# Weight conversions tied to their item and spread over the items; query and key tests loaded four steps ahead

## The chip, the cores and the metric

The kernel runs on one core of one Trainium2 chip. The metric is the device time of one launch in microseconds; before the change it is 623.04 us, the median of 3 runs (622.54 to 623.23).

## The reference

What is computed is a sparse causal attention followed by two feed-forward layers, all in float32. There are 2 batches, 8 heads, 768 positions and 64 columns a head; 1536 tokens of 512 columns enter each layer, with 2048 hidden columns.

```python
scores = q @ k.T / sqrt(D) + bias            # local window of 96 and 8 global keys
x = softmax(where(keep, scores, -1e9)) @ v   # -> 1536 x 512
h = x @ moe_w_in                             # layer 0
g = maximum(h, 0) + log1p(exp(-abs(h)))
x = g @ moe_w_out
h = x @ moe2_w_in                            # layer 1
out = (h * clip(h + 3, 0, 6) / 6) @ moe2_w_out
```

The weights arrive as 64-bit floats, which the kernel reads as pairs of 32-bit words.

## The kernel before

**Items.** Each layer's 2048 hidden columns are cut into 16 chunks of 128, and the chunks into phases of 6, 5 and 5 (PHASES). Within a phase the loop goes over three groups of 512 tokens, and within a group over the phase's chunks. One pass, a chunk times a token group, is an *item* (`item`, L362): 12 matrix products make h from x and the chunk's input weights, `split_g` (L264) applies the layer's function on ScalarE and VectorE and splits the result into a high and a low part (gh, gl), and 12 products add it into four accumulators. Each factor is a sum of two reduced-precision parts, so a product is made of three (`matmul3`, L296). An item is named by four digits: layer, phase, group, chunk within the phase. Four banks hold h, so TensorE can make the h of later items while an earlier item's g is still being formed.

**Units.** A chunk's input weights and its output weights are each one *unit*, 64 in all; wa9_1 belongs to chunk 9, half 1. `unit_load` (L186) issues the unit's 512 KB DMA into a tile raw, of which four exist. `unit_convert` (L201) turns the words into float32 and splits them: Abs on ScalarE (L219), a clamp on GpSimd (L220), three bit operations on VectorE (L221, L224, L227), a copy on ScalarE (L231, the high part), a subtraction on VectorE (L232, the low part). Twelve units are converted beside the attention in a shorter way. From unit 12 on, `run` (L457) calls `weight_step(1)` (L249) once behind each item: one more unit, if a slot for its chunk is free. Eleven slots hold weights; in a phase's last token group each item frees its chunk's slot.

**Tests.** From the second phase of layer 1 on, `run` also calls `check_step` (L730): 36 steps that test whether the inputs are in the range that this path allows. Twelve (`range_step`, L234) load a unit of weights again and reduce it on VectorE with four operations (L243 to L247); 24 load 128 rows of q or k, 256 KB, and square and sum them on ScalarE (L747). All use the tiles raw. At the end a flag is made that decides whether a general path runs again; it does not here. The last token group (`last_items`, L408) makes all its h first (hz0 to hz4), calls four test steps behind each, and only then accumulates.

**Order.** Each engine takes its instructions in program order, and that order is set when the program is built: the framework places every instruction by its own estimate of when its inputs are ready. In the attention and the products of the first layer that run beside it a table (ORDER) fixes it; behind that it is free. So a unit's work that was called behind an item may stand many items earlier in an engine's queue, as far as slots and raw tiles allow.

Of the kernel before, what the change touches and what calls it, by code (L numbers as in the profile page):

```python
# [21 lines left out]
KC = DM // P  # L22
NCH = DFF // P
PHASES = ((6, 5, 5), (6, 5, 5))
FIRST_SLOTS, MORE_SLOTS = 6, 5
CW = 512
GT, GB = 256, 512
# [23 lines left out]
def r32(ap):  # L51
    return ap.bitcast(F32)
# [81 lines left out]
class Layers:  # L134
# [6 lines left out]
    def __init__(self, ctx, tc, weights, three, xsh, xsl, out):  # L141
        self.ctx, self.tc, self.nc = ctx, tc, tc.nc
        self.weights, self.xsh, self.xsl, self.out = weights, xsh, xsl, out
        self.pool("mp", 2)
        self.pool("tp", 5)
        self.pool("pp", 1)
        self.part = [self.pp.tile([P, 4, GB], F32, name=f"part{g}") for g in range(T // GB)]
        self.three = three
        self.W, self.raws, self.slot = {}, {}, {}
        self.done, self.loaded = 0, 0  # L150
        first = range(PHASES[0][0])
        early = range(2 * EARLY_PAIRS)
        self.order = [(j, u) for js in (early, first[len(early):]) for u in range(2) for j in js]
        self.order += [(j, u) for j in range(len(first), 2 * NCH) for u in range(2)]
        self.free, self.h_tags, self.acc_tags, self.wr = [], [], [], []
        self.room, self.hint, self.bare = None, False, 0
        self.plan, self.mark = None, lambda label, made: made
        self.n_h, self.halves, self.in_first, self.beside = 0, 0, True, False
        self.grow(0, FIRST_SLOTS, 2, 2)
# [41 lines left out]
    def unit_convert(self, x):  # L201

        nc = self.nc
        j, u = self.order[x]
        if u == 0:
            self.slot[j] = self.free.pop(0)
            wp, t = self.slot[j]
            self.W[j] = [wp.tile([P, CW], F32R, tag=f"w{i}_{t}", name=f"w{i}_{j}") for i in range(4)]
        raw = self.raws.pop(x)
        hi, lo = raw[:, :, 1], raw[:, :, 0]  # L210
        z = self.home(x, 6)
        if z < 4:
            a = self.part[2][:, z, :]
        else:
            a = self.wr[x % len(self.wr)].tile([P, CW], F32, tag="wa", name=f"wa{j}_{u}")
        ai = a.bitcast(I32)
        bare = x < self.bare
        if not bare:
            nc.scalar.activation(a, raw.bitcast(F32)[:, :, 1], AF.Abs)  # L219
            nc.gpsimd.tensor_scalar(out=a, in0=a, scalar1=W_HI, scalar2=W_LO, op0=ALU.min, op1=ALU.max)  # L220
        self.mark(f"u{x}.0", nc.vector.tensor_scalar(  # L221
            out=ai, in0=hi if bare else ai, scalar1=3, scalar2=0x3FFFFFF8, op0=ALU.logical_shift_left, op1=ALU.bitwise_and
        ))
        self.mark(f"u{x}.1", nc.vector.scalar_tensor_tensor(  # L224
            out=ai, in0=hi, scalar=-2 ** 30, in1=ai, op0=ALU.bitwise_and, op1=ALU.bitwise_or
        ))
        self.mark(f"u{x}.2", nc.vector.scalar_tensor_tensor(  # L227
            out=ai, in0=lo, scalar=29, in1=ai, op0=ALU.logical_shift_right, op1=ALU.bitwise_or
        ))
        wh, wl = self.W[j][2 * u:2 * u + 2]  # L230
        self.mark(f"w{x}", nc.scalar.copy(wh, a))  # L231
        self.mark(f"u{x}.3", nc.vector.tensor_tensor(out=wl, in0=a, in1=r32(wh), op=ALU.subtract))  # L232

    def range_step(self, x, m):  # L234

# [126 lines left out]
    def item(self, layer, ph, G, s):  # L362

        nc = self.nc
        xsh, xsl, part = self.xsh[G], self.xsl[G], self.part[G]
        W = self.W[layer * NCH + sum(PHASES[layer][:ph]) + s]
        wih, wil = (t.rearrange("p (k c) -> p k c", k=KC) for t in W[0:2])
        woh, wol = W[2:4]
        n = f"{layer}{ph}{G}{s}"
        h = self.h_bank(f"h{n}")  # L370
        for call in self.matmul3(
            h, [((wih[:, c], wil[:, c]), (xsh[:, c, :], xsl[:, c, :])) for c in range(KC)], True, True
        ):
            call()
        gh, gl = self.split_g(layer, h, n)
        first_s, last_s = s == 0, s == PHASES[layer][ph] - 1
        first_ph, last_ph = ph == 0, ph == len(PHASES[layer]) - 1
        if first_s:
            self.acc = [self.bank(t, f"acc{n}{i}") for i, t in enumerate(self.acc_tags)]
        for m in range(4):  # L380
            ms = slice(m * P, (m + 1) * P)
            acc, pm = self.acc[m], part[:, m, :]
            if layer == 0:
                pair = ((woh[:, ms], wol[:, ms]), (gh, gl))
            else:
                pair = ((gh[:, ms], gl[:, ms]), (woh, wol))
            for call in self.matmul3(acc, [pair], first_s, last_s):
                call()
            if not last_s:
                continue  # L390
            if layer == 0:
                if first_ph:
                    nc.scalar.copy(pm, acc)
                    continue
                nc.vector.tensor_tensor(out=pm, in0=acc, in1=pm, op=ALU.add)
                if last_ph:
                    nc.scalar.copy(xsh[:, m, :], pm)
                    nc.vector.tensor_tensor(out=xsl[:, m, :], in0=pm, in1=r32(xsh[:, m, :]), op=ALU.subtract)
                continue
            if first_ph:  # L400
                nc.scalar.mul(pm, acc, 1.0 / 6.0)
                continue
            nc.vector.scalar_tensor_tensor(out=pm, in0=acc, scalar=1.0 / 6.0, in1=pm, op0=ALU.mult, op1=ALU.add)
            if last_ph:
                t0 = G * GB + m * P
                nc.sync.dma_start(out=self.out[t0:t0 + P, :], in_=pm)

    def last_items(self, ph, G, spare_step):  # L408
# [3 lines left out]
        if self.hint:  # L412
            self.tc.mark_branch_hint_location("redo", engines=list(mybir.ALL_ENGINES))
        g, W = [], []
        for s in range(PHASES[1][ph]):
            W.append(self.W[NCH + sum(PHASES[1][:ph]) + s])
            wih, wil = (t.rearrange("p (k c) -> p k c", k=KC) for t in W[s][0:2])
            h = self.h_bank(f"hz{s}")
            for call in self.matmul3(
                h, [((wih[:, c], wil[:, c]), (self.xsh[G][:, c, :], self.xsl[G][:, c, :])) for c in range(KC)], True, True  # L420
            ):
                call()
            wp, t = self.free.pop(0)
            where = [wp.tile([P, CW], F32R, tag=f"w{i}_{t}", name=f"g{i}_{s}") for i in range(2)]
            g.append(self.split_g(1, h, f"z{s}", where))
            for _ in range(4):
                spare_step()
        for m in range(4):
            acc = self.bank(self.acc_tags[m], f"accz{m}")
            t0 = G * GB + m * P  # L430
# [26 lines left out]
    def run(self, att=None, spare_step=lambda: None):  # L457
# [32 lines left out]
        self.plan, self.mark = None, lambda label, made: made  # L490
        self.grow(1, MORE_SLOTS, 2, 2)
        self.in_first = False
        for layer in range(2):
            for ph, chunks in enumerate(PHASES[layer]):
                for G in range(T // GB - 1 if layer == 0 and ph == 0 else 0, T // GB):
                    if layer == 1 and ph == len(PHASES[1]) - 1 and G == T // GB - 1:
                        self.last_items(ph, G, spare_step)
                        continue
                    for s in range(chunks):
                        self.item(layer, ph, G, s)  # L500
                        if G == T // GB - 1:
                            self.release(layer, ph, (s,))
                        self.weight_step(1)
                        if layer == 1 and ph:
                            spare_step()


# [17 lines left out]
def fast_path(tc, ident, three, nf, counts, q, k, qt, kt, v, weights, out, flag):  # L525


    with ExitStack() as ctx, ExitStack() as actx:
# [196 lines left out]
                return step["v"] == quads  # L725

        chk = {}
        todo = list(range(-layers.bare, 2 * B * NB))

        def check_step():  # L730

            if not todo:
                return
            fp = layers.wr[1]
            if not chk:
                chk["sq"] = fp.tile([P, 2 * B * NB], F32, name="sq")
                chk["wm"] = fp.tile([P, layers.bare, 2], F32, name="wm")
            sq, wm = chk["sq"], chk["wm"]
            t = todo.pop(0)
            if t < 0:  # L740
                layers.range_step(t + layers.bare, wm)
                return
            z, n = divmod(t, B * NB)
            x = layers.wr[t % 2].tile([P, CW, 2], I32, tag="raw", name=f"chk{t}").bitcast(F32)
            x = x.rearrange("p c t -> p (c t)")[:, 0:DM]
            nc.sync.dma_start(out=x, in_=(q, k)[z][n * P:(n + 1) * P, :])
            nc.scalar.activation(x, x, AF.Square, accum_out=sq[:, t:t + 1])  # L747
            if todo:
                return
            m1 = fp.tile([P, 1], F32, name="m1")  # L750
            nc.vector.tensor_reduce(out=m1, in_=sq, axis=AX.X, op=ALU.max)
# [217 lines left out]
```

## Time and profile before

| what | value |
|---|---|
| median of 3 runs | 623.04 us |
| profiled execution, its own time | 622.77 us |
| its span (first to last instruction) | 621.0 us |
| TensorE busy | 611.2 us, 98% of the span |
| VectorE, ScalarE, GpSimd busy | 447.7, 375.0, 136.2 us |
| granted TensorE clock, mean | 0.999 |

The profiled execution lies 0.27 us under the median; 1.77 us of its time lie around the span. Busy time of TensorE is modelled: products are pipelined, and one of 512 columns is shown as 0.39 us long, while the next may start much sooner. Whether TensorE loses time is therefore read from the starts of its products, or from how many of them start in a window. On the other engines too the next instruction may start a little before the one shown ends.

### The profile page before, as it was taken

Reading aid. Unit: us, or ns where it says so; the run is one execution under the profiler, and the core shown is the slowest. Engines: PE = TensorE matmul, PEld = TensorE weight load, DVE = VectorE, ACT = ScalarE, POOL = GpSimd, SP = SyncE. Lnnn points to the kernel's source line nnn. Section 1 sums busy time; section 2 is a strip of 40 time slices with the busy share of each in tenths; the row PEclk is TensorE's granted clock in tenths of the full one; section 3 lists DMA queues with packets and bytes.
Section 4 is the critical chain, followed back from the end, with each engine's and each line's share of the span. In section 5 each row is a group of like instructions: output and inputs, shape, how many; then the busy total and the mean of one; then the engine's idle time right before and its main releaser. Section 6 shows DMA issues by size and latency. Waiting matters only on the chain.

```text
span 621.0 us, 9444 instructions
## 1 busy us (share of the span) xinstructions
PE 611.2 (98%) x3350; PEld 507.4 (82%) x3352; DVE 447.7 (72%) x945; ACT 375.0 (60%) x795; POOL 136.2 (22%) x169
## 2 busy tenths in 40 slices
PE   8999999999999999999999999999999999999997
PEld 4789888999778887888888888888888878888886
DVE  8989676649999999999878995226999442424162
ACT  6998689676887977786767752326545642222230
POOL 3855344434233333332001410001100000000000
PEclk9999999999999999999999999999999999999999
DMA  8583203014533433323101341001656610001011
GB/s 267 184 284 112 73 1 112 6 57 170 169 117 121 136 136 102 103 102 109 61 0 35 101 137 69 0 1 40 200 196 207 188 52 0 1 0 69 0 69 70
DMA packets 26803, 59.90 MB, mean 96 GB/s; under 512 B 2688, under 2 KB 9344, under 8 KB 26752
## 3 DMA queue, kind: packets, MB, share of 16 engines
q1 hardware_dynamic: 26752, 59.26, 28.6%
q8 instruction: 27, 0.44, 0.3%
q14 instruction: 24, 0.20, 0.1%
HBM read 56.10 MB, written 3.15 MB: 95 GB/s over the span
## 4 chain that ended last, share of the span: by engine, by line
PE 66%; DVE 18%; DMA 8%; ACT 4%; issue 3%; POOL 0%; SPq 0%; ACTq 0%; POOLq 0%
PE acc L301 23%; PE h L301 21%; PE hf L301 5%; PE accf L301 3%; PE s L629 3%; PE px L683 3%; PE ptp L665 3%; DVE wa L227 3%; DVE wa L224 3%; PE accz L301 2%; DMA chk<-in_q 2%; DMA chk<-in_k 2%; PE hz L301 2%; DVE w L232 2%; DVE gl L293 2%
## 5 line engine op out<-in xcount | busy, mean ns | idle before, releaser
L301 PE MATMUL h<-xsh,w 128*128 128x512 f32 x632 | 167.3, 390 | 0.9 <-DVE t L285 0.8
L301 PEld LDWEIGHTS h<-xsh,w 128*128 128x128 f32 x632 | 118.0, 188 | 27.3 <-DVE t L285 3.1
L220 POOL TENSOR_SCALAR wa<-wa 128x512 f32<-128x512 f32 x52 | 70.2, 1354 | 240.7 <-ACT wa L219 240.6
L301 PE MATMUL acc<-w,gh 128*128 128x512 f32 x344 | 106.0, 389 | 0.0
L301 PE MATMUL acc<-gh,w 128*128 128x512 f32 x288 | 92.0, 390 | 0.2 <-ACT gh L292 0.2
L293 DVE TENSOR_TENSOR gl<-t,gh 128x512 fp32r<-128x512 f32 x79 | 55.0, 696 | 48.4 <-ACT gh L292 48.3
L301 PE MATMUL h<-xsl,w 128*128 128x512 f32 x316 | 86.7, 389 | 0.0
L292 ACT CAST gh<-t 128x512 fp32r<-128x512 f32 x79 | 49.0, 620 | 56.2 <-PE acc L301 38.0
L301 PEld LDWEIGHTS acc<-w,gh 128*128 128x128 f32 x344 | 64.6, 188 | 13.4
L290 ACT ACTIVATE t<-h,three 128x512 f32<-128x512 f32 x43 | 29.5, 687 | 72.3 <-PE h L301 70.5
L291 DVE SCALAR_TENSOR_TENSOR t<-t,h 128x512 f32<-128x512 f32 x43 | 29.4, 684 | 55.9 <-ACT t L290 55.8
L301 PEld LDWEIGHTS h<-xsl,w 128*128 128x128 f32 x316 | 59.2, 188 | 12.4
L301 PE MATMUL acc<-w,gl 128*128 128x512 f32 x172 | 67.2, 391 | 1.3 <-DVE gl L293 1.3
L520 POOL TENSOR_SCALAR pm<-pm,rs 128x256 f32<-128x256 f32 (+1 forms) x96 | 57.0, 609 | 43.6 <-DVE rs L518 25.4
L301 PEld LDWEIGHTS acc<-gh,w 128*128 128x128 f32 x288 | 53.9, 188 | 12.4 <-ACT gh L292 1.0
L301 PE MATMUL acc<-gl,w 128*128 128x512 f32 x144 | 56.0, 389 | 0.0
L640 ACT ACTIVATE pm<-pm,nm 128x256 f32<-128x256 f32 (+1 forms) x96 | 46.6, 488 | 3.5 <-DVE nm L635 3.5
L219 ACT ACTIVATE wa<-raw 128x512 f32<-128x512 f32 x52 | 35.0, 673 | 14.6 <-DVE w L232 6.0
L635 DVE CUSTOM_DVE_ANT_0 pm<-s,bias 128x256 f32<-128x256 f32 (+1 forms) x96 | 35.1, 394 | 10.2 <-PE s L629 9.9
L231 ACT CAST w<-wa 128x512 fp32r<-128x512 f32 x56 | 34.5, 617 | 12.4 <-PE acc L301 8.7
L301 PE MATMUL accf<-ghf,w 128*128 128x256 f32 x192 | 41.8, 299 | 0.0
L232 DVE TENSOR_TENSOR w<-wa,w 128x512 fp32r<-128x512 f32 x56 | 38.8, 695 | 3.3 <-ACT w L231 3.3
(122 smaller groups left out, 1032.5 us busy)
## 6 DMA issues: line engine op xcount, KB each, us to landing
raw<-in_w2i SPq DMA_DIRECT2D x16, 512.0 KB, 3.2
raw<-in_w2o SPq DMA_DIRECT2D x16, 512.0 KB, 3.2
raw<-in_w1i SPq DMA_DIRECT2D x14, 512.0 KB, 4.0
raw<-in_w1o SPq DMA_DIRECT2D x12, 512.0 KB, 3.2
V<-in_v SPq DMA_DIRECT2D x12, 256.0 KB, 3.4
range<-in_w1i SPq DMA_DIRECT2D x6, 512.0 KB, 4.0
range<-in_w1o SPq DMA_DIRECT2D x6, 512.0 KB, 3.9
chk<-in_q SPq DMA_DIRECT2D x12, 256.0 KB, 3.1
```

The costliest lines, as they stand in the source:

```text
L219: nc.scalar.activation(a, raw.bitcast(F32)[:, :, 1], AF.Abs)
L220: nc.gpsimd.tensor_scalar(out=a, in0=a, scalar1=W_HI, scalar2=W_LO, op0=ALU.min, op1=ALU.max)
L231: self.mark(f"w{x}", nc.scalar.copy(wh, a))
L232: self.mark(f"u{x}.3", nc.vector.tensor_tensor(out=wl, in0=a, in1=r32(wh), op=ALU.subtract))
L290: nc.scalar.activation(t1, hf, AF.Relu, bias=self.three[:, 0:1])
L291: nc.vector.scalar_tensor_tensor(out=t3, in0=t1, scalar=6.0, in1=hf, op0=ALU.min, op1=ALU.mult)
L292: mark(f"h{n}", nc.scalar.copy(gh, t3))
L293: mark(f"L{n}", nc.vector.tensor_tensor(out=gl, in0=t3, in1=r32(gh), op=ALU.subtract))
L301: return self.nc.tensor.matmul(out, lhsT=a, rhs=b, start=start and z == 0, stop=stop and z == len(seq) - 1, **kw)
L520: mark("N", nc.gpsimd.tensor_scalar(out=t, in0=t, scalar1=rs[:, j:j + 1], scalar2=0.0, op0=ALU.mult, op1=ALU.add))
L635: mark(f"T{k}.{z}", nc.vector.tensor_tensor_reduce(out=pmz, in0=ps[z % 2][:, z // 2, 0:nsl, :].rearrange("p s t -> p (s t)"), in1=bias[:, ...
L640: mark(f"e{k}.{z}", nc.scalar.activation(pmz, pmz, AF.Exp, bias=nm[:, z:z + 1], scale=-1.0, accum_out=sm[:, z:z + 1]))
```

## The change

A unit's Abs (L219 of the kernel before) and the square of a q or k test are given an order behind the first of the 12 products of the item that they were called behind. This is no wait on the chip: no semaphore is added, it only keeps the build from placing them further ahead. A rule (`wanted`) lets a unit be called only when its share of the items up to the phase that needs it has passed: one per item in the first 15 items, then about two in three, with layer 1's last ones one per item again. Test steps begin when all units are done. Range tests and q/k tests alternate, and a q or k load is asked for four q/k steps before its square.

```diff
@@ unit_convert
-            nc.scalar.activation(a, raw.bitcast(F32)[:, :, 1], AF.Abs)
+            made = nc.scalar.activation(a, raw.bitcast(F32)[:, :, 1], AF.Abs)
+            if self.anchor:
+                self.behind(made, self.anchor)
...
+    def behind(self, made, one):
+        info = mybir.DependencyInfo(mybir.DependencyClass.NoSync, mybir.DependencyReason.DATA)
+        self.tc.add_manual_dep(made.ins, one.name, info, reason="order")
@@ item, and last_items for each hz
-            call()
+            made = call()
+            self.anchor = self.anchor or made.ins
@@ run
+        items = [(layer, ph, G, s) for layer in range(2) for ph, c in enumerate(PHASES[layer])
+                 for G in range(T // GB) for s in range(c)]
+        dues = [(k, 2 * (layer * NCH + sum(PHASES[layer][:ph]) + s + 1) + 1)
+                for k, (layer, ph, G, s) in enumerate(items) if G == 0 and s == PHASES[layer][ph] - 1]
+        def wanted(*item):
+            k = items.index(item) + 1
+            for (a, m), (b, n) in zip(dues, dues[1:]):
+                if a <= k < b and items[b][:2] <= (1, 0):
+                    return m + (n - m) * (k - a) / (b - a)
+            return 4 * NCH
...
+                        self.anchor = None
                         self.item(layer, ph, G, s)
...
-                        self.weight_step(1)
-                        if layer == 1 and ph:
+                        self.weight_step(1 if self.done < wanted(layer, ph, G, s) else 0)
+                        if layer == 1 and ph and self.done == 4 * NCH:
                             spare_step()
@@ check_step
-        todo = list(range(-layers.bare, 2 * B * NB))
+        ranges, todo, asked = list(range(layers.bare)), list(range(2 * B * NB)), []
...
-            t = todo.pop(0)
-            if t < 0:
-                layers.range_step(t + layers.bare, wm)
+            if ranges and 2 * B * NB - len(todo) >= layers.bare - len(ranges):
+                layers.range_step(ranges.pop(0), wm)
                 return
...
+            while todo and len(asked) < CHECK_AHEAD:
+                t = todo.pop(0)
...
+                nc.sync.dma_start(out=x, in_=(q, k)[z][n * P:(n + 1) * P, :])
+                asked.append((t, x))
+            t, x = asked.pop(0)
+            made = nc.scalar.activation(x, x, AF.Square, accum_out=sq[:, t:t + 1])
+            if layers.anchor:
+                layers.behind(made, layers.anchor)
```

How queues change is shown at three places; line numbers of the new program are 3 to 29 higher.

VectorE between the low parts of items 0021 and 0022, before (t1 to t3 are `split_g`'s tiles; w1 and w3 are the low parts of a chunk's input and output weights):

```order
L293 TENSOR_TENSOR gl0021_2365<-t30021_2367,gh0021_2364 128x512
L224 SCALAR_TENSOR_TENSOR wa11_0_2865<-raw11_0_2704,wa11_0_2865 128x512
L221 TENSOR_SCALAR wa10_1_2808<-wa10_1_2808 128x512
L227 SCALAR_TENSOR_TENSOR wa10_0_2759<-raw10_0_2598,wa10_0_2759 128x512
L232 TENSOR_TENSOR w3_9_2656<-wa9_1_2706,w2_9_2655 128x512
L288 TENSOR_TENSOR t30022_2416<-t30022_2416,t20022_2417 128x512
L227 SCALAR_TENSOR_TENSOR wa11_0_2865<-raw11_0_2704,wa11_0_2865 128x512
L282 SCALAR_TENSOR_TENSOR t20023_2470<-t20023_2470,t10023_2468 128x512
L285 SCALAR_TENSOR_TENSOR t30023_2469<-h0023_16_2453,t30023_2469 128x512
L224 SCALAR_TENSOR_TENSOR wa10_1_2808<-raw10_1_2651,wa10_1_2808 128x512
L232 TENSOR_TENSOR w1_10_2756<-wa10_0_2759,w0_10_2755 128x512
L293 TENSOR_TENSOR gl0022_2414<-t30022_2416,gh0022_2413 128x512
```

and now:

```order
L301 TENSOR_TENSOR gl0021_2365<-t30021_2367,gh0021_2364 128x512
L230 SCALAR_TENSOR_TENSOR wa8_0_2547<-raw8_0_2390,wa8_0_2547 128x512
L296 TENSOR_TENSOR t30022_2416<-t30022_2416,t20022_2417 128x512
L227 SCALAR_TENSOR_TENSOR wa8_1_2600<-raw8_1_2439,wa8_1_2600 128x512
L290 SCALAR_TENSOR_TENSOR t20023_2470<-t20023_2470,t10023_2468 128x512
L293 SCALAR_TENSOR_TENSOR t30023_2469<-h0023_16_2453,t30023_2469 128x512
L235 TENSOR_TENSOR w1_8_2544<-wa8_0_2547,w0_8_2543 128x512
L224 TENSOR_SCALAR wa9_0_2657<-wa9_0_2657 128x512
L230 SCALAR_TENSOR_TENSOR wa8_1_2600<-raw8_1_2439,wa8_1_2600 128x512
L301 TENSOR_TENSOR gl0022_2414<-t30022_2416,gh0022_2413 128x512
```

Before, VectorE worked here at units of chunks 9, 10 and 11; now at those of chunks 8 and 9, and two rows fewer stand between the two low parts.

ScalarE in the tests, before, items 1111 to 1113 (sq takes a square's sum):

```order
L292 CAST gh1111_5281<-t31111_5284 128x512
L290 ACTIVATE t11112_5323<-h1112_74_5308,three_70 128x512
L747 ACTIVATE chk11_5965,sq_5023<-chk11_5965 128x512
L747 ACTIVATE chk13_6038,sq_5023<-chk13_6038 128x512
L290 ACTIVATE t11113_5363<-h1113_75_5348,three_70 128x512
L747 ACTIVATE chk15_6044,sq_5023<-chk15_6044 128x512
L747 ACTIVATE chk17_6071,sq_5023<-chk17_6071 128x512
L292 CAST gh1112_5321<-t31112_5324 128x512
L747 ACTIVATE chk19_6077,sq_5023<-chk19_6077 128x512
L747 ACTIVATE chk21_6104,sq_5023<-chk21_6104 128x512
L292 CAST gh1113_5361<-t31113_5364 128x512
```

and now, items 1114 to 1123:

```order
L300 CAST gh1114_5375<-t31114_5378 128x512
L298 ACTIVATE t11120_5421<-h1120_77_5406,three_70 128x512
L776 ACTIVATE chk2_5237,sq_5187<-chk2_5237 128x512
L300 CAST gh1120_5419<-t31120_5422 128x512
L298 ACTIVATE t11121_5461<-h1121_78_5446,three_70 128x512
L300 CAST gh1121_5459<-t31121_5462 128x512
L298 ACTIVATE t11122_5501<-h1122_79_5486,three_70 128x512
L776 ACTIVATE chk3_5239,sq_5187<-chk3_5239 128x512
L300 CAST gh1122_5499<-t31122_5502 128x512
L298 ACTIVATE t11123_5537<-h1123_80_5522,three_70 128x512
L300 CAST gh1123_5535<-t31123_5538 128x512
```

Between two casts (gh) stood two to four squares; now it is one or none, and a square's load is asked for four squares earlier.

VectorE in the range tests, before, items 1102 and 1103 (wm takes the maxima):

```order
L293 TENSOR_TENSOR gl1102_5094<-t31102_5096,gh1102_5093 128x512
L246 SCALAR_TENSOR_TENSOR rangea10_5471<-rangea10_5471 128x512
L243 TENSOR_SCALAR rangea7_5343<-range7_5341 128x512
L247 TENSOR_REDUCE wm_5024<-rangea8_5383 128x1
L246 SCALAR_TENSOR_TENSOR rangea5_5263<-rangea5_5263 128x512
L293 TENSOR_TENSOR gl1103_5146<-t31103_5148,gh1103_5145 128x512
L247 TENSOR_REDUCE wm_5024<-rangea10_5471 128x1
L244 TENSOR_REDUCE wm_5024<-rangea7_5343 128x1
L291 SCALAR_TENSOR_TENSOR t31104_5196<-t11104_5195,h1104_71_5180 128x512
L247 TENSOR_REDUCE wm_5024<-rangea5_5263 128x1
```

and now, items 1114 and 1120:

```order
L255 TENSOR_REDUCE wm_5188<-rangea1_5277 128x1
L251 TENSOR_SCALAR rangea3_5357<-range3_5355 128x512
L301 TENSOR_TENSOR gl1114_5376<-t31114_5378,gh1114_5375 128x512
L252 TENSOR_REDUCE wm_5188<-rangea3_5357 128x1
L254 SCALAR_TENSOR_TENSOR rangea3_5357<-rangea3_5357 128x512
L255 TENSOR_REDUCE wm_5188<-rangea3_5357 128x1
L251 TENSOR_SCALAR rangea5_5481<-range5_5479 128x512
L252 TENSOR_REDUCE wm_5188<-rangea5_5481 128x1
L299 SCALAR_TENSOR_TENSOR t31120_5422<-t11120_5421,h1120_77_5406 128x512
L254 SCALAR_TENSOR_TENSOR rangea5_5481<-rangea5_5481 128x512
L255 TENSOR_REDUCE wm_5188<-rangea5_5481 128x1
L301 TENSOR_TENSOR gl1120_5420<-t31120_5422,gh1120_5419 128x512
```

Before, the operations of four range tests were mixed with those of the items; now a test's first operation stands right behind the last of the test before it, and the items' operations behind that.

## Rows read from the trace of the kernel before

**Rows 1.** The page, span and busy time by engine.

```profile
span 621.0 us, 9444 instructions
PE 611.2 (98%) x3350; PEld 507.4 (82%) x3352; DVE 447.7 (72%) x945; ACT 375.0 (60%) x795; POOL 136.2 (22%) x169
```

**Rows 2.** Windows of 20 us; columns: stretch, length, busy (instructions) per engine, clock, DMA.

```profile
156.00:176.00 20.00, 19.55 (x83) 15.06 (x83) 19.07 (x33) 16.30 (x30) 4.11 (x5) 1.00 0.49 158
176.00:196.00 20.00, 20.00 (x89) 16.24 (x88) 20.00 (x35) 16.03 (x28) 6.73 (x5) 1.00 0.37 127
...
216.00:236.00 20.00, 19.98 (x88) 16.06 (x86) 19.62 (x34) 15.16 (x27) 7.12 (x5) 1.00 0.31 105
236.00:256.00 20.00, 19.41 (x84) 15.56 (x84) 20.00 (x36) 15.83 (x28) 9.08 (x4) 1.00 0.40 132
...
416.00:436.00 20.00, 20.00 (x89) 16.54 (x89) 12.22 (x21) 11.44 (x20) 1.85 (x3) 1.00 0.16 53
...
476.00:496.00 20.00, 20.00 (x90) 16.57 (x89) 10.54 (x19) 13.65 (x36) 0.00 (x0) 1.00 0.60 184
496.00:516.00 20.00, 18.74 (x82) 14.81 (x81) 8.56 (x16) 7.87 (x17) 0.00 (x0) 1.00 0.14 41
```

**Rows 3.** Who waited for whom, TensorE: total us, times, longest.

```profile
PE acc L301 <- DVE gl L293: 1.3, 2, 0.7
PE h L301 <- DVE t L285: 0.8, 2, 0.6
...
PE accf L301 <- DVE glf L293: 0.4, 1, 0.4
```

**Rows 4.** The chain that ended last, in order of time: start, us, what.

```profile
245.54 2.72 PE acc L301 x12
```

**Rows 5.** VectorE, groups by shape, 160 to 300 us.

```profile
L224 DVE SCALAR_TENSOR_TENSOR wa<-raw,wa 128x512 int32<-128x512 int32 x31 | 21.8, 704 | 0.0
...
L282 DVE SCALAR_TENSOR_TENSOR t<-t,t 128x512 f32<-128x512 f32 x27 | 18.8, 697 | 0.8 <-ACT t L281 0.8
```

**Rows 6.** VectorE in order of time; columns: start, duration, instruction, [idle before].

```profile
152.25 0.68 DVE L293 TENSOR_TENSOR glf<-t3f,ghf 128x512 fp32r<-128x512 f32 x1
...
164.43 0.68 DVE L285 SCALAR_TENSOR_TENSOR t<-h,t 128x512 f32<-128x512 f32 x1
165.03 0.68 DVE L227 SCALAR_TENSOR_TENSOR wa<-raw,wa 128x512 int32<-128x512 int32 x1
...
170.43 0.41 DVE L221 TENSOR_SCALAR wa<-wa 128x512 int32<-128x512 int32 x1
170.77 0.68 DVE L293 TENSOR_TENSOR gl<-t,gh 128x512 fp32r<-128x512 f32 x1
```

**Rows 7.** ScalarE in order of time, same columns.

```profile
493.75 0.67 ACT L290 ACTIVATE t<-h,three 128x512 f32<-128x512 f32 x1
495.25 0.63 ACT L747 ACTIVATE chk<-chk 128x512 f32<-128x512 f32 x1 [0.83 <-DMA chk<-in_k]
...
496.64 0.63 ACT L747 ACTIVATE chk<-chk 128x512 f32<-128x512 f32 x1 [0.67 <-DMA chk<-in_k]
...
497.27 0.60 ACT L292 CAST gh<-t 128x512 fp32r<-128x512 f32 x1
```

**Rows 8.** TensorE in order of time, around the same stall.

```profile
498.65 0.50 PE L301 MATMUL acc<-w,gl 128*128 128x512 f32 x1 [0.60 <-DVE gl L293]
```

**Rows 9.** TensorE in order of time, first full item.

```profile
155.82 1.09 PE L301 MATMUL h<-xsl,w 128*128 128x512 f32 x4
```

**Rows 10.** The tile chk: waits for it, and issue to landing.

```profile
  ACT chk L747: 13.1, 14
...
DMA to landing us min/median/max: 2.5/2.8/4.0
```

**Rows 11.** The tile range: issue to landing.

```profile
DMA to landing us min/median/max: 3.1/4.0/5.1
```

**Rows 12.** The tile raw: issue to landing.

```profile
DMA to landing us min/median/max: 3.1/3.2/7.7
```

More of the change, by code (lines that the diff above doesn't have):

```diff
@@ L24 @@
 PHASES = ((6, 5, 5), (6, 5, 5))
+CHECK_AHEAD = 4
 FIRST_SLOTS, MORE_SLOTS = 6, 5
@@ L155, in __init__ @@
         self.free, self.h_tags, self.acc_tags, self.wr = [], [], [], []
-        self.room, self.hint, self.bare = None, False, 0
+        self.room, self.hint, self.bare, self.anchor = None, False, 0, None
         self.plan, self.mark = None, lambda label, made: made
@@ L421, in last_items @@
             ):
-                call()
+                made = call()
+                self.anchor = self.anchor or made.ins
             wp, t = self.free.pop(0)
@@ L427, in last_items @@
                 spare_step()
+            self.anchor = None
         for m in range(4):
@@ L499, in run @@
                     for s in range(chunks):
+                        self.anchor = None
                         self.item(layer, ph, G, s)
@@ L727, in fast_path @@
         chk = {}
-        todo = list(range(-layers.bare, 2 * B * NB))
+        ranges, todo, asked = list(range(layers.bare)), list(range(2 * B * NB)), []
         def check_step():
-            if not todo:
+            if not todo and not asked:
                 return
@@ L738, in check_step @@
             sq, wm = chk["sq"], chk["wm"]
-            t = todo.pop(0)
-            if t < 0:
-                layers.range_step(t + layers.bare, wm)
+            if ranges and 2 * B * NB - len(todo) >= layers.bare - len(ranges):
+                layers.range_step(ranges.pop(0), wm)
                 return
[L743 to L748, printed above, removed]
+            while todo and len(asked) < CHECK_AHEAD:
+                t = todo.pop(0)
+                z, n = divmod(t, B * NB)
+                x = layers.wr[t % 2].tile([P, CW, 2], I32, tag="raw", name=f"chk{t}").bitcast(F32)
+                x = x.rearrange("p c t -> p (c t)")[:, 0:DM]
+                nc.sync.dma_start(out=x, in_=(q, k)[z][n * P:(n + 1) * P, :])
[4 more added lines that the diff above has]
+                layers.behind(made, layers.anchor)
+            if todo or asked:
                 return
```

## The prediction

> **What bounds the kernel now.** I began with the page: TensorE is busy in 611.2 of 621.0 us [rows 1], so there seems to be nothing to gain but 10 us. Behind the attention every product of 512 columns has the same rhythm: 12 in 2.72 us [rows 4], 0.2267 us each, so that an item of 24 takes 5.44 us. At this rhythm a window of 20 us shows 89 or 90 products (the one cut at its edge included), as in 476 to 496 [rows 2]; of the 22 windows from 156 to 596 us 15 show 90 and seven fewer. The clock is at its upper level, 2.4 GHz, throughout (1.00 in each of these rows). So only missing starts can be won back, and they lie in two places [rows 2]:
>
> - 156 to 256 us: 83, 89, 89, 88 and 84 products; against 90 that is 7 + 1 + 1 + 2 + 6 = 17, or 17 x 0.2267 = 3.85 us (196 to 216 reads as 176 to 196). A wait of 0.4 us just before (accf for glf, [rows 3]) belongs to it: 4.2 us.
> - 496 to 516 us: 82, so 8 x 0.2267 = 1.8 us.
>
> Together 6.0 us. A window can read one off by where it is cut (416 to 436 shows 89 and has no wait), so I give that sum 0.5 us either way.
>
> The list of waits names what ends them [rows 3]: VectorE's gl, its t (the read that frees a bank of h), and glf. In the first place VectorE is busy 19 to 20 of 20 us [rows 2], an operation of 512 elements every 0.60 us and the integer shift every 0.34 [rows 6]. A unit costs it 0.34 + 3 x 0.60 = 2.14 us, an item of layer 0 4 x 0.60 = 2.4: together 4.54 of the 5.44 that TensorE needs, so one unit an item would fit. But between 160 and 300 us it begins 31 units for 27 items [rows 5], and they do not wait their turn: the queue was filled with units of chunks that are far from needed, and the item's own four operations stand behind them. In the second place VectorE is not busy (8.56 of 20). ScalarE is held up there: the square at 496.64 waited 0.67 us for its DMA, the one before 0.83, and the cast of gh behind them ran only at 497.27 [rows 7], so that TensorE waited 0.60 for gl [rows 8]. Squares waited 13.1 us for DMA in all [rows 10].
>
> **Part 1: units behind their item's first product, and spread.** No instruction is added or dropped; 52 units and their 52 DMAs stay. What moves: in VectorE's queue, from the last operation of the first products (glf at 152.25 [rows 6]) to the low part of item 0112, stood 152 operations, 89 of them units'; now 127, 63 of them units'. Those 25 fewer are at 0.57 us ((0.34 + 3 x 0.60) / 4 is 0.54, an item's 0.60) some 14 us taken out of the 89 us that end with the wait near 241, where TensorE lost most at once. They come back between 256 and 420 us, where VectorE had idle time in the old run (12.22 of 20 in 416 to 436 [rows 2]) and TensorE loses nothing. Of the waits in this place I therefore expect all to go: **-4.2 us**. The bounds: nothing, if the queue is late for another reason; 4.2 is all that there is.
>
> What is late next? Weights. The nearest case is chunk 10, whose input half is needed by item 0104. In TensorE's new queue 176 products lie between the first of item 0021 (155.82 + 8 x 0.2267 = 157.6 [rows 9]) and the first of 0104: 39.9 us, 197.5. In VectorE's new queue 66 operations lie between glf and that chunk's low part, 10 at 0.34 and 56 at 0.60: 37.0 us behind 152.85, 189.9. That leaves 7.6 us for its waits on ScalarE, GpSimd and DMA. Chunks 11 and later have over 20 us. A raw tile is asked for three units, some 16 us, ahead and lands in 3.2 (median) to 7.7 us [rows 12], so SP's queue, in which loads now stand in order of units, is no limit. On GpSimd only the 52 clamps move.
>
> The Trainium skill, Perfetto Trace Analysis, "Optimization Strategy", speaks against this part: where an engine has gaps one should "determine how to make those dependencies start sooner, or complete faster", and the tie makes a unit's start later. The trace does not agree with that section of the Trainium skill here: where units start soonest, TensorE waits [rows 2, 3]. By the rule the time would be that of the fourth rival below.
>
> **Part 2: squares with loads asked for early.** A load of q or k lands in 2.8 us (2.5 to 4.0 [rows 10]); four steps are about four items, 21.8 us. In the new queue of ScalarE a square stands between a cast and the next, each 0.63 us (496.64 to 497.27 [rows 7]), and no longer waits: **-1.8 us**. Bounds: 0 and 1.8. Squares come bunched only at the end: the last 15, called four behind each hz. Eight of them stand ahead of the cast for item 1214. The first four have their data; the second four are asked for as the first are done, at least 5 us before ScalarE reads h of 1214. From the end of that h TensorE has 43 products, 9.7 us, before it needs gl; Relu, four squares, cast and subtraction take 0.67 + 4 x 0.63 + 0.60 + 0.68 = 4.5. Cover: 5 us. The last squares stand ahead of the cast for hz1, whose h ends 46 products (10.4 us) before the flag's transpose in TensorE's new queue, and item outputs that stand behind q/k loads in SP's queue end nothing.
>
> **Part 3: range tests, now in a row.** Each next load waits until VectorE has read the last one. At items 1113 to 1121 four run in series: Relu and square (0.67 + 0.63), four times landing L and a first operation of 0.34, then five of 0.60 up to gl of 1121: 5.7 + 4 L. TensorE needs that gl 110 products, 24.9 us, behind the end of h of 1113. So up to L = 4.8 us nothing waits; it was 4.0 (3.1 to 5.1 [rows 11]). I take 0; with 5.1 each time it costs 1.2 us.
>
> **Sum.** 622.77 - 4.2 - 1.8 = 616.8 us for the profiled execution; the median stood 0.27 us above it, so **617.0 us**.
>
> **Rivals.**
> 1. *The ramp keeps its waits.* From 152 to 176 us four raw tiles, GpSimd and the first units are chained whatever their order; then the 7 products (1.59 us) and 0.4 us stay, 2.0 us: 619.0. For it: this is the window that loses most [rows 2], and it stands at the start of the units. Against: the new queue has glf ahead of all full units.
> 2. *VectorE stays late* in the whole first stage, as unit and item still fill 4.54 of 5.44 us; only the squares gain: 623.04 - 1.8 = 621.2. Against: the 25 operations that went.
> 3. *Order is all that changes, and the waits come back elsewhere*: no gain, 623.0. The queue rows speak against it.
> 4. *Weights come late.* Were VectorE's queue 10 us late by its waits instead of under 7.6, item 0104 waits 2.4 us: 619.4. Against: this is the one chunk with so little lead. The rule of the Trainium skill named above points to this case.
> 5. *Slower: range loads in series.* VectorE stands still behind each, with gl and t of items in its queue. Beyond L = 4.8 us each load costs four times the excess; at 7.7 us (the longest raw load [rows 12]) 5.7 + 30.8 - 24.9 = 11.6 us: 628.6. It decides from 5.7 + 4 L = 24.9 + 7.3, L = 6.6 us. Against: 5.1 was the longest of twelve, at a DMA share of 0.60 [rows 2].
>
> **How the numbers follow.** Forecast 0.60, ramp 0.18, VectorE late 0.08, no gain 0.05, weights 0.05, slower 0.04. The forecast's own bounds are 616.5 to 617.5; the range takes in the ramp and the weights, to 619.4, and 0.1 below: 616.4 to 619.4. A measurement tells 0.2%, 1.25 us, from no change; under 621.8 is faster. That is the first three cases and the weights, 0.91; I say 0.90, with 0.06 for within 0.2% and 0.04 for slower.
>
> **What would show it.** Right: windows of 20 us with 89 or 90 products from 160 to 590 us; VectorE with idle time before 256 us; squares with no DMA wait ahead of a cast that TensorE waits for; about 615 us of span. Wrong: products missing in 156 to 176 (rival 1), waits of h on L235's low part w (rival 4), idle VectorE ended by a DMA of range with TensorE waiting for gl (rival 5).

## The result and the profile after

| | before | with the change |
|---|---|---|
| median | 623.13 us (6 runs, 622.54 to 624.51) | 616.85 us (6 runs, 616.23 to 618.25) |
| ratio | | 0.9899, 95% interval 0.9883 to 0.9915 |
| profiled execution, its own time | 622.77 us | 617.12 us |
| its span | 621.0 us | 615.3 us |
| first product into a full-size h, start | 147.73 us | 147.91 us |
| last product, start | 616.51 us | 610.76 us |
| between the two | 468.77 us | 462.85 us |

The forecast was 617.0 us. The last row of the table is the yardstick of what follows: it leaves out the attention, where the change moves nothing but a few operations of units at its end, and which alone varies by 2 us from one execution to another (below). It shrank by 5.92 us; the prediction counted 6.0 us of missing starts.

The page after, span and busy time, beside [rows 1]:

```profile
span 615.3 us, 9412 instructions
PE 607.8 (99%) x3352; PEld 507.9 (83%) x3352; DVE 454.9 (74%) x945; ACT 371.2 (60%) x795; POOL 117.1 (19%) x169
```

VectorE's busy time did not fall, it rose by 7 us. The work is the same; where it stands in the queue is not.

Windows of 20 us after, in the columns of [rows 2]:

```profile
156.00:176.00 20.00, 20.00 (x90) 16.56 (x89) 19.47 (x32) 17.87 (x32) 6.79 (x6) 1.00 0.31 105
176.00:196.00 20.00, 20.00 (x90) 16.53 (x90) 19.49 (x34) 16.47 (x29) 8.05 (x4) 1.00 0.30 106
...
216.00:236.00 20.00, 20.00 (x90) 16.57 (x89) 18.56 (x31) 13.04 (x22) 2.84 (x3) 1.00 0.24 79
236.00:256.00 20.00, 20.00 (x90) 16.57 (x89) 15.37 (x26) 12.62 (x23) 1.28 (x2) 1.00 0.15 54
...
416.00:436.00 20.00, 20.00 (x90) 16.56 (x89) 14.76 (x24) 10.33 (x19) 2.90 (x4) 1.00 0.27 99
...
476.00:496.00 20.00, 20.00 (x90) 16.57 (x89) 8.90 (x16) 5.17 (x9) 0.00 (x0) 1.00 0.09 30
496.00:516.00 20.00, 20.00 (x90) 16.57 (x89) 16.88 (x29) 6.80 (x13) 0.00 (x0) 1.00 0.39 133
```

Every window has its 89 or 90 products, where [rows 2] had 83, 84 and 82 in the three worst. VectorE is still busy 19.5 of 20 us from 156 to 216, so a nearly full VectorE alone was not what cost the time. What moved is the place of the items' operations in its queue. The gl of item 0025 and the first product that reads it, before:

```profile
198.08 0.68 DVE L293 TENSOR_TENSOR gl<-t,gh 128x512 fp32r<-128x512 f32 x1
```

```profile
200.16 0.39 PE L301 MATMUL acc<-gl,w 128*128 128x512 f32 x1
```

and now:

```profile
191.33 0.68 DVE L301 TENSOR_TENSOR gl<-t,gh 128x512 fp32r<-128x512 f32 x1
```

```profile
195.31 0.39 PE L309 MATMUL acc<-gl,w 128*128 128x512 f32 x1
```

It was the 75th VectorE operation behind glf and is the 63rd. Its lead, from its end to that product, grew from 1.4 to 3.3 us.

Who waited for whom, TensorE, after, beside [rows 3]:

```profile
PE s L655 <- DMA qT<-in_qt: 1.3, 1, 1.3
PE warm L808 <- DVE zeros L576: 1.3, 1, 1.3
PE ptp L691 <- ACT pm L666: 0.3, 1, 0.3
PE ptp L691 <- ACT pT L693: 0.2, 1, 0.2
```

gl, t and glf are gone from the list; what is left belongs to the start and the attention.

### The profile page after: what moved, and what is told of

The parts are those of the page before. It is cut to its first block, busy times and chain, and to the rows that moved or that the text cites. A ratio compares the mean times of both kernels' runs of the same rounds, so it can differ in the third digit from the quotient of the medians.

```text
span 615.3 us, 9412 instructions
## 1 busy us (share of the span) xinstructions
PE 607.8 (99%) x3352; PEld 507.9 (83%) x3352; DVE 454.9 (74%) x945; ACT 371.2 (60%) x795; POOL 117.1 (19%) x169
## 4 chain that ended last, share of the span: by engine, by line
PE 96%; ACT 2%; DMA 1%; issue 0%; SPq 0%; DVE 0%
PE h L309 35%; PE acc L309 35%; PE hf L309 6%; PE accf L309 6%; PE px L709 4%; PE s L655 3%; PE ptp L691 3%; PE accz L309 2%; PE hz L309 2%; ACT pm L666 1%; DMA qT<-in_qt 1%; ACT pT L693 0%; PE warm L808 0%; SPq L582 0%; SPq L581 0%
## 5 line engine op out<-in xcount | busy, mean ns | idle before, releaser
L223 POOL TENSOR_SCALAR wa<-wa 128x512 f32<-128x512 f32 x52 | 50.0, 963 | 263.3 <-ACT wa L220 259.8
L309 PE MATMUL acc<-gh,w 128*128 128x512 f32 x288 | 93.5, 389 | 0.0
L546 POOL TENSOR_SCALAR pm<-pm,rs 128x256 f32<-128x256 f32 (+1 forms) x96 | 58.3, 623 | 42.5 <-DVE rs L544 24.0
L227 DVE SCALAR_TENSOR_TENSOR wa<-raw,wa 128x512 int32<-128x512 int32 x53 | 38.4, 725 | 0.7
```

The lines of the kernel that those rows point to most:

```text
L227: self.mark(f"u{x}.1", nc.vector.scalar_tensor_tensor(out=ai, in0=hi, scalar=-2 ** 30, in1=ai, op0=ALU.bitwise_and, op1=ALU.bitwise_or))
L309: return self.nc.tensor.matmul(out, lhsT=a, rhs=b, start=start and z == 0, stop=stop and z == len(seq) - 1, **kw)
L546: mark("N", nc.gpsimd.tensor_scalar(out=t, in0=t, scalar1=rs[:, j:j + 1], scalar2=0.0, op0=ALU.mult, op1=ALU.add))
```

## The experiments

All ratios are to the kernel before, run on the same chip beside the kernel. "Length" is the last row of the table above, taken from the one profiled execution of each. By the starts of its products the kernel before lost 4.0 us in the first place (up to 256 us) and 1.9 us in the second (near 500).

| kernel | ratio (95% interval) | length, us |
|---|---|---|
| before | 1 | 468.77 |
| the change | 0.9899 (0.9883 to 0.9915) | 462.85 |
| the change again | 0.9925 (0.9901 to 0.9950) | 462.85 |
| a_tie: units' tie alone | 0.9934 (0.9916 to 0.9953) | 463.47 |
| b_spread: spreading alone | 1.0017 (1.0002 to 1.0033) | 471.23 |
| c_tests: tests' part alone | 0.9972 (0.9959 to 0.9986) | 466.21 |
| f_sqfree: without the squares' tie | 0.9975 (0.9954 to 0.9996) | 465.09 |
| d_ask1: loads not asked early | 0.9916 (0.9894 to 0.9937) | 462.85 |
| j_ties: the two ties alone | 0.9916 (0.9895 to 0.9936) | 462.85 |
| dose1: +1 VectorE operation a unit | 0.9929 (0.9910 to 0.9948) | 464.33 |
| dose3: +3 VectorE operations a unit | 1.0346 (1.0324 to 1.0369) | 489.79 |
| range2: range loads twice as long | 0.9945 (0.9925 to 0.9964) | 463.35 |
| k_late: tie 2.5 us later | 0.9923 (0.9897 to 0.9948) | 462.96 |
| lat3: units slower on GpSimd | 1.0418 (1.0385 to 1.0451) | 494.07 |

### Which part wins the first place

**a_tie**, the kernel before with the edit below (`behind`, and the lines that set the anchor, are as in the change and left out here):

```diff
-            nc.scalar.activation(a, raw.bitcast(F32)[:, :, 1], AF.Abs)
+            made = nc.scalar.activation(a, raw.bitcast(F32)[:, :, 1], AF.Abs)
+            if self.anchor:
+                self.behind(made, self.anchor)
```

> Only the tie of the units; no spreading, tests as before. Theory A (the tie alone wins the first place, since it takes 23 of the units' operations out of VectorE's queue between glf and the low part of item 0112, 66 instead of 89, where the full change has 63): TensorE's products of 156 to 256 us come back, 4.2 us; the squares still stand two to eight between casts, so the 1.8 us near 500 stay: 618.9 us, ratio 0.993. Rival B (the spreading wins it): 623.1, ratio 1.000.

**b_spread**, the kernel before with the edit below (`wanted` is as in the change and left out here):

```diff
-                        self.weight_step(1)
-                        if layer == 1 and ph:
+                        self.weight_step(1 if self.done < wanted(layer, ph, G, s) else 0)
+                        if layer == 1 and ph and self.done == 4 * NCH:
```

> Only the spreading of the units over the items (tests in their old order, begun when the units are done); no tie. VectorE's queue has 153 operations, 89 of them units', between glf and the low part of item 0112, as before. Theory A: no gain, 623.1 us, ratio 1.000, products missing in 156 to 256 us as before. Rival B: 618.9, ratio 0.993.

Windows of a_tie:

```profile
156.00:176.00 20.00, 20.00 (x90) 16.57 (x89) 19.50 (x33) 17.85 (x31) 6.80 (x6) 1.00 0.29 105
...
236.00:256.00 20.00, 20.00 (x90) 16.57 (x89) 18.43 (x31) 13.87 (x25) 2.40 (x4) 1.00 0.23 80
...
496.00:516.00 20.00, 19.71 (x87) 15.98 (x86) 8.06 (x17) 10.00 (x24) 0.00 (x0) 1.00 0.32 97
```

and of b_spread:

```profile
156.00:176.00 20.00, 19.65 (x84) 15.27 (x83) 19.28 (x33) 16.51 (x29) 3.92 (x5) 1.00 0.48 158
...
236.00:256.00 20.00, 19.43 (x83) 15.37 (x84) 20.00 (x35) 15.91 (x28) 9.17 (x4) 1.00 0.37 132
...
496.00:516.00 20.00, 17.37 (x75) 13.74 (x75) 7.96 (x15) 8.52 (x18) 0.00 (x0) 1.00 0.18 54
```

The tie alone brings back every product of the first place. Near 500 us it keeps a loss of 0.6 us, where 1.8 were expected to stay: the kernel is 5.3 us shorter and not 4.2, and the ratio, which came out at the expected 0.993, does not show that difference. The spreading alone brings back none in the first place and loses more near 500 (two waits for gl, 2.6 us; squares wait 17.2 us for their loads instead of 13.1); why it loses more there was not followed up. A rule on when a unit is *called* won nothing here while the build could still place the called unit further ahead.

### Which part wins the second place

**c_tests**, the change without the units' tie and with one unit an item, as before; tests begin in the second phase (`@@ run` marks a cut):

```diff
-            made = nc.scalar.activation(a, raw.bitcast(F32)[:, :, 1], AF.Abs)
-            if self.anchor:
-                self.behind(made, self.anchor)
+            nc.scalar.activation(a, raw.bitcast(F32)[:, :, 1], AF.Abs)
@@ run
-                        self.weight_step(1 if self.done < wanted(layer, ph, G, s) else 0)
-                        if layer == 1 and ph and self.done == 4 * NCH:
+                        self.weight_step(1)
+                        if layer == 1 and ph:
```

> Only the tests: alternating, loads asked for four steps ahead, squares tied; units as before. Theory A: the 1.8 us near 500 go and the 4.2 us of 156 to 256 stay: 621.3 us, ratio 0.997; no cast of gh behind a square that waited for its DMA. Rival (the range tests in series take the gain back): 623.1 or above, with TensorE waiting for gl while VectorE waits for range. Tests begin five items earlier here than in the full change, while units still run.

It went as the theory has it near 500 us: ratio 0.9972, and no missing product after 242 us. The first place keeps most of its loss, 3.4 us instead of 4.0:

```profile
156.00:176.00 20.00, 19.82 (x87) 15.62 (x86) 19.93 (x34) 16.73 (x29) 4.47 (x5) 1.00 0.45 156
```

By the tiles' names, the first 169 operations behind glf on VectorE and behind ghf on ScalarE stand in the order of the kernel before. In the trace of the kernel before VectorE waits there once for ScalarE, in that of c_tests it does not:

```profile
162.61 0.69 DVE L232 TENSOR_TENSOR w<-wa,w 128x512 fp32r<-128x512 f32 x1 [0.90 <-ACT w L231]
```

So a kernel's waits can differ by some 0.6 us from one execution to another, and a difference of that size between two lengths is not by itself the effect of an edit.

**f_sqfree**, the change with

```diff
-            if layers.anchor:
-                layers.behind(made, layers.anchor)
```

in the test step, 

> The whole change without the tie of the squares; loads are still asked for four steps ahead. ScalarE's queue has one to five squares between casts again, four and five of them at items 1110 and 1111. Theory C (what won the second place is that squares no longer bunch, and the tie does that): squares wait for DMA ahead of casts again, up to 1.8 us lost, 617.5 to 618.7 us. Rival D (the early asking does it): 616.9 us, no wait of TensorE after 440 us.

**d_ask1**, the change with

```diff
-CHECK_AHEAD = 4
+CHECK_AHEAD = 1
```

> The whole change with each q or k load asked for right ahead of its square (one step instead of four); the squares keep their tie, one between two casts up to item 1212. Theory C (the tie spreads the squares, and SP issues each load as soon as a tile is free, so it lands in 2.8 us long before the square's turn): as the changed kernel, ratio 0.990, no wait of TensorE after 440 us. Rival D (the early asking is needed): squares wait for DMA at most steps, and up to 1.8 us come back, ratio 0.993.

f_sqfree asks for its loads four steps early and waits for them more than the kernel before did. The tile chk in f_sqfree, who waited for it (us, times):

```profile
  ACT chk L776: 22.6, 15
```

ScalarE in f_sqfree, in order of time, as [rows 7]:

```profile
509.31 0.63 ACT L776 ACTIVATE chk<-chk 128x512 f32<-128x512 f32 x1 [1.21 <-DMA chk<-in_k]
...
510.81 0.63 ACT L776 ACTIVATE chk<-chk 128x512 f32<-128x512 f32 x1 [0.78 <-DMA chk<-in_k]
...
511.44 1.12 ACT L300 CAST gh<-t 128x512 fp32r<-128x512 f32 x2
```

and TensorE there, as [rows 8]:

```profile
512.82 0.50 PE L309 MATMUL acc<-w,gl 128*128 128x512 f32 x1 [1.75 <-DVE gl L301]
```

Five squares stand between the cast before, at 503.18, and this one. There are four tiles raw: once four loads are under way, the next one has to wait for a square (this is read from the code and not measured). With the tie and without early asking (d_ask1) squares wait 1.7 us in all, in three places, and TensorE never. So the tie of the squares won the second place, and asking early won nothing measurable. With that tie the change, c_tests, d_ask1 and j_ties lose nothing there. Without it the loss is 0.6 us (a_tie), 1.9 (before), 2.2 (f_sqfree) or 3.2 (b_spread): what it is worth depends on where the rest stands.

**j_ties**, the kernel before with the units' tie of a_tie and, in the test step (what sets the anchor is again left out),

```diff
-            nc.scalar.activation(x, x, AF.Square, accum_out=sq[:, t:t + 1])
+            made = nc.scalar.activation(x, x, AF.Square, accum_out=sq[:, t:t + 1])
+            if layers.anchor:
+                layers.behind(made, layers.anchor)
```

> The kernel before with the two ties alone: no spreading, range tests first and in a row of twelve, loads not asked for early. Theory: VectorE's queue has 66 units' operations up to the low part of 0112 and one or two squares stand between two casts, so both places are won: ratio 0.990, some 617 us. Rival (the other parts are needed to keep the tests from bunching): the range tests now stand twelve in a row among items 1100 to 1113, and TensorE waits there for gl, 1 to 3 us: ratio 0.992 to 0.995.

Its length is that of the change, and VectorE's order behind glf is that of the change for the first 113 operations. The twelve range tests in a row fill VectorE, and TensorE loses nothing; a window of j_ties:

```profile
456.00:476.00 20.00, 20.00 (x89) 16.54 (x89) 20.00 (x39) 6.18 (x10) 0.43 (x1) 1.00 0.60 199
```

The rival that the other parts are needed falls: two ties win all that the change wins.

### How much room is left

**dose1** and **dose3**, the change with n = 1 or 3 more low parts made behind each unit's own:

```diff
+        if not self.in_first:
+            nc.vector.tensor_tensor(out=wl, in0=a, in1=r32(wh), op=ALU.subtract)
```

> The whole change, and each unit of the 52 makes its low part twice: one more operation of 0.60 us on VectorE a unit, 31 us in all, so unit and item need 5.14 of 5.44 us instead of 4.54. If a queue in the right order has room (the low parts of units lead their product by 7 us or more, gl by 5): nothing lost, ratio 0.990; by sums over the new queue the least lead is then 2.7 us. If VectorE is at its bound: up to 31 us, at least as many as before the change, ratio above 1.000.

> The same with three more operations a unit: 94 us more on VectorE, unit and item need 6.34 us where TensorE takes 5.44. Then VectorE is the bound as long as there is one unit an item, whatever the order: 0.9 us an item over 15 items is 13.5 us, and by sums over the new queue the lateness grows to 20 us: 630 to 637 us, ratio 1.011 to 1.022. If it stays at 0.990, VectorE's load was never what TensorE waited for.

dose1 lost 464.33 - 462.85 = 1.5 us, in one wait, where none was expected. Its list of waits:

```profile
PE acc L311 <- DVE gl L303: 1.1, 1, 1.1
```

The wait is for gl of item 0025, the very item that had the least lead by the sums, 2.7 us:

```profile
192.85 0.68 DVE L303 TENSOR_TENSOR gl<-t,gh 128x512 fp32r<-128x512 f32 x1
```

```profile
193.58 0.50 PE L311 MATMUL acc<-gl,w 128*128 128x512 f32 x1 [1.15 <-DVE gl L303]
```

Summed as in the prediction (behind 152.85, 66 operations, 9 of them at 0.34 us and 57 at 0.60), this gl ends at 190.1; it ended at 193.5, 3.4 us later. On the way VectorE waited 3.2 us and lost 3.5 more in operations that took longer than these figures; glf, 3.3 us sooner than the sum has it, made up for half of that. A lateness of 3.4 us is more than the cover of 2.7. In the changed kernel the same gl was 3.9 us later than its sum and had the room: 3.3 us were left of some 7. dose3 lost 26.9 us, more than the 13.5 to 20 expected, in waits that end from 180 to 380 us:

```profile
PE h L313 <- DVE t L297: 9.9, 12, 1.8
PE acc L313 <- DVE gl L305: 5.4, 3, 2.5
PE acc L313 <- ACT gh L304: 2.1, 4, 0.7
```

So VectorE's amount of work does bind a little above the present one: one more operation a unit costs 1.5 us and three cost 26.9. At the present amount it does not, and before the change it was the order.

**k_late**, the change with, in `item`,

```diff
-            self.anchor = self.anchor or made.ins
+            self.anchor = made.ins
```

> The whole change with units tied behind the last instead of the first of their item's 12 products, 11 x 0.2267 = 2.5 us later. In the changed kernel the least lead of a weight is that of chunk 10, 3.3 us by its trace. Theory: leads fall by at most 2.5 us and nothing is lost: ratio 0.990. Rival (weights come late): TensorE waits for a low part w near 197 us, up to 2 us, ratio 0.993.

This moves the squares' tie along with the units'. No wait followed. The lead of chunk 10's low part, the least of a weight, is 1.8 us by the trace instead of 3.3. Starting units later still cost nothing here, where a lead was left.

**lat3**, the change with the clamp repeated:

```diff
             nc.gpsimd.tensor_scalar(out=a, in0=a, scalar1=W_HI, scalar2=W_LO, op0=ALU.min, op1=ALU.max)
+            for _ in range(0 if self.in_first else 3):
+                nc.gpsimd.tensor_scalar(out=a, in0=a, scalar1=W_HI, scalar2=W_LO, op0=ALU.min, op1=ALU.max)
```

> The whole change with the clamp of a unit on GpSimd made four times instead of once, so that a unit takes longer and VectorE's work stays the same. By sums over the new queue the low parts of chunks 7, 9 and 10 lead their product by 0 to 1 us, where those of the changed kernel led by 7 to 12 and the trace showed 3.3 to 9.5. If weights can become the bound (the fourth rival): 3 to 5 us are lost between 176 and 236 us, ratio 0.995 to 0.998, and TensorE waits for w or for gl behind it. If nothing waits for them: 0.990.

It lost 494.07 - 462.85 = 31.2 us, six times the upper end of what was expected. Its waits:

```profile
PE h L311 <- DVE t L295: 7.7, 2, 4.0
PE h L311 <- DVE t L301: 5.4, 4, 2.2
PE h L311 <- DVE w L237: 3.9, 4, 1.2
PE acc L311 <- DVE w L237: 1.9, 1, 1.9
```

Weights are waited for (w, 5.8 us in 5 waits), and operations of items (t, 13.1 us in 6), whose causes were not followed up one by one. The experiment changed more than one thing: the build placed h products and units differently, so it shows that the fourth rival's wait exists, not its price for the change. A second cost came with the waits. TensorE in lat3 in order of time, and windows of 4 us:

```profile
224.99 2.08 PE L311 MATMUL h<-xsh,w 128*128 128x512 f32 x4 [3.67 <-DVE t L295]
226.86 1.91 PE L311 MATMUL h<-xsl,w 128*128 128x512 f32 x4
228.57 1.91 PE L311 MATMUL h<-xsh,w 128*128 128x512 f32 x4
```

```profile
220.00:224.00 4.00, 1.31 (x6) 0.75 (x4) 0.71 (x1) 3.74 (x7) 3.13 (x6) 1.00 0.00 0
224.00:228.00 4.00, 3.01 (x7) 2.44 (x8) 3.96 (x6) 3.65 (x7) 4.00 (x6) 0.54 0.00 0
228.00:232.00 4.00, 4.00 (x12) 3.11 (x12) 3.95 (x6) 3.38 (x6) 1.01 (x1) 0.61 0.00 0
232.00:236.00 4.00, 4.00 (x19) 3.30 (x19) 2.48 (x4) 3.04 (x6) 0.00 (x0) 1.00 0.00 0
```

At a wait of 3.67 us the granted clock fell to its lower level, 1.2 GHz: four products in 1.71 us (226.86 to 228.57), 0.43 each instead of 0.2267, until 231. The same is seen behind three more waits, of 1.9 to 4.0 us. In all 38 products ran so, which is 7.5 of the 31.2 us.

**range2**, the change with each range load issued twice:

```diff
         nc.sync.dma_start(out=raw.rearrange("p c t -> p (c t)"), in_=self.weights[2 * layer + u][f])
+        nc.sync.dma_start(out=raw.rearrange("p c t -> p (c t)"), in_=self.weights[2 * layer + u][f])
```

> The whole change, with each range test's load of 512 KB issued twice into the same tile, one behind the other, so that it lands in about 6.2 us instead of 3.1. This prices the slower rival: by the prediction's formula four in series take 5.7 + 4 x 6.2 = 30.5 us where TensorE gives 24.9, so 5.6 us are lost near 500 to 520 us, ratio 0.999. If the series is not a bound because one item's operations and not four stand behind each load (in the new queue of this kernel gl of 1114, 1120 and 1121 stand behind one load each): nothing or under 1 us, ratio 0.990.

The length is 463.35, so 0.5 us lost, in one wait for gl at 524 us; VectorE waits 15.6 us for the tile range instead of 11.1. The formula's 5.6 us did not come. The build, which knows of the second load, placed the items' operations differently (one item's behind each load), so this prices a longer load in a queue made for it, and not a load that is late in the queue of the change. That case was not tried.

**The change again**, unchanged. 

> The changed kernel once more, beside the others, for the scatter: ratio 0.990, and from the first product of the first full item to the last product 462.9 us, whatever the stretch ahead of it takes.

Length 462.85, as in the first profile; its ratio, 0.9925, has an interval that overlaps the first.

## Why the prediction was right, point by point

- **What bounds.** Right. 6.0 us of missing starts were counted, and 5.92 us came off between the first full-size product and the last. 621.0 - 5.92 + 0.18 (the later start of that stretch) = 615.3, the span. By place it was 4.0 us instead of 4.2, and 1.9 instead of 1.8. That the medians agree to 0.15 us is partly luck: the profiled execution took 617.12 us, 0.35 more than the 616.77 of the sum, and stood 0.27 above its median, where the forecast had it 0.27 below.
- **Part 1, -4.2 us.** Right in mechanism and, to 0.2 us, in size; too wide in what it credits. "52 units ... behind their item's first product, and spread" was costed as one; the tie alone wins all of the first place (a_tie), the spreading nothing there (b_spread, j_ties). The count of queue rows told this already: 66 of units' operations up to the low part of 0112 with the tie alone, 63 with both, 89 with the spreading alone.
- **What is late next: chunk 10's weights.** Right in the place, with less room than the sum says. It gave 7.6 us "for its waits on ScalarE, GpSimd and DMA"; 3.3 us were left. Low part and product of the change, from VectorE and TensorE in order of time:

```profile
193.14 0.68 DVE L235 TENSOR_TENSOR w<-wa,w 128x512 fp32r<-128x512 f32 x1
```

```profile
197.12 1.07 PE L309 MATMUL h<-xsh,w 128*128 128x512 f32 x4
```

  193.14 + 0.68 = 193.8 against 197.1; forecast were 189.9 and 197.5. So VectorE was 3.9 us later than the sum. The sum also began in the wrong place, with the end that glf had in the kernel before, 152.85; in the changed kernel no operation of a full unit stands ahead of glf on VectorE, and it ended 3 us sooner:

```profile
149.28 0.69 DVE L301 TENSOR_TENSOR glf<-t3f,ghf 128x512 fp32r<-128x512 f32 x1 [0.74 <-ACT ghf L300]
```

  From there VectorE took 6.9 us more than 37.0: 3.9 in waits, the longest of 2.28 us for a clamp on GpSimd, and 3.0 in operations that took longer than 0.60 and 0.34 us. Two errors partly made up for each other, and 3.3 us of the cover remained.
- **The rule weighed in part 1.** The Trainium skill (Perfetto Trace Analysis, "Optimization Strategy") would make the dependencies that an engine waits for start sooner. Read on gl, t and glf, for which TensorE waited, the trace agrees: these now come sooner (the gl of 0025 ends at 192.0 instead of 198.8 us), because units that are not yet due stand behind them. The prediction read the rule on the units, and so read, it does not hold here: 2.5 us later (k_late) cost nothing measurable, and the fourth rival did not come. lat3 is a case in which a later unit does cost: there TensorE waited 5.8 us for weights.
- **Part 2, -1.8 us.** Right in size; the text put early asking and the spacing of the squares into one step, and only the spacing counts. "Between a cast and the next" stood one square, with the tie, up to the bunch at the end; without it up to five, with early asking (f_sqfree). That squares "no longer wait" was nearly so: they waited 1.7 us in two places, and no wait of TensorE followed. Of the squares bunched at the end none held TensorE up.
- **Part 3, 0.** Right: L was 3.1 us (3.1 to 4.4), under the 4.8 from which it would cost, and VectorE's 11.1 us of waits for the tile range ended in no wait of TensorE. The formula's price beyond that point was not confirmed (range2).
- **Rivals.** The ramp kept no wait: its products depended on the order after all, as a_tie's 90 products in 156 to 176 show. VectorE stayed as full as the second rival says up to 216 us, and TensorE lost nothing.

## What to carry to other kernels

An in-order engine that is nearly full hurts when work that is not yet needed stands ahead of work that is; look at whose operations stand between two due ones before calling the engine the bound. Where the build may place work freely, tell it in the order (here a tie without a wait on the chip), since limits on when a step is called, or a load asked for, won nothing here. A lead summed from durations along a queue leaves out the engine's own waits and its slower operations: in dose1 the sum came out 3.4 us too early, enough to turn a cover of 2.7 us into a wait of 1.1.

## What the runs showed that was not expected

**The clamp on GpSimd stretches.** Forms are the same, durations are 0.61 to 3.71 us in the change. GpSimd in order of time:

```profile
155.96 0.61 POOL L223 TENSOR_SCALAR wa<-wa 128x512 f32<-128x512 f32 x1
...
175.93 3.71 POOL L223 TENSOR_SCALAR wa<-wa 128x512 f32<-128x512 f32 x1 [0.83 <-ACT wa L220]
```

and VectorE at the short one, and at the end of the long one:

```profile
156.03 0.82 DVE L224 TENSOR_SCALAR wa<-wa 128x512 int32<-128x512 int32 x1 [2.28 <-POOL wa L223]
...
178.49 0.68 DVE L235 TENSOR_TENSOR w<-wa,w 128x512 fp32r<-128x512 f32 x1
179.68 0.43 DVE L224 TENSOR_SCALAR wa<-wa 128x512 int32<-128x512 int32 x1 [0.51 <-POOL wa L223]
```

The short one ran beside an operation of one input tile. The long one ran while VectorE had five operations of two input tiles one behind another, from 176.08 to 179.17, and ended at 179.64, when VectorE had run out and was waiting for it. The Trainium skill (SBUF — State Buffer, "Who interferes with whom") says that a VectorE instruction with two inputs in SBUF contends with a GpSimd instruction that reads SBUF. The rows agree, though spans on GpSimd are rough and no run tested it alone. The wait of 0.51 us at 179.68 is part of what the sums left out.

**The attention varies from execution to execution.** The first full-size product starts at 147.4 to 147.9 us in ten of the 14 profiles, at 148.3 in lat3 and at 149.2 to 149.9 in f_sqfree, d_ask1 and j_ties. The change alone has spans of 614.4 to 616.5 us in its six executions. From 10 to 20 us DMA moved 283 GB/s in the change's profile and 232 in that of d_ask1. What decides it stays open; it is why lengths are given beside the ratios for kernels that differ by 1 us.
